# Score products one couple ahead of their transposed partners, and two late pieces of the last group moved

## The chip, the cores and the metric

The kernel runs on one core of a Trainium2 chip. The metric is the device time of one launch in microseconds, the median of several runs; profiles are of one execution. The engines are PE (matrix products), DVE, ACT and POOL (elementwise work) and SP (transfers only), and PE's matrix array can be used as one block of 128 rows or, for operands that span 64 partitions, as two halves of 64 rows. In this text L is the half of rows 0 to 63 and U that of rows 64 to 127.

## The reference

```python
S, D, H, Dh, W, F = 2048, 512, 32, 16, 256, 1792

q, k, v = split_heads(x @ wqkv)                      # 32 heads of 16
scores = einsum("bhqd,bhkd->bhqk", q, k) * Dh**-0.5
mask = (i - j >= 0) & (i - j < W)                    # sliding block
p = softmax(where(mask, scores, -1e9))
a = merge_heads(einsum("bhqk,bhkd->bhqd", p, v)) @ wo

b = (silu(x @ w_gate) * (x @ w_up)) @ w_down

g = sigmoid((x * gate_w).sum(-1, keepdims=True))
out = g * a + (1 - g) * b
```

## The kernel before

Float32 operands are split into two parts, hi and lo, and each product is made of three (hi by hi, hi by lo, lo by hi). A prologue makes v and the projections q and k. A last stage multiplies the hidden tiles by `w_down` and the attention's output by `wo`. The change lies in the stage between, which runs attention and the products with `w_gate` and `w_up` side by side.

That stage goes through the 32 heads in 8 groups of 4. It has 128 blocks t (16 per group, one for each 128 queries), and each block has four couples hd = 0 to 3; a couple is the unit of its order, number 4t + hd. In a couple the loop at L796 issues, in this order:

- one score product of the next group (L593, `stage1`, a generator that yields after each): queries by keys, 384 columns wide, from which DVE takes the row maxima (L595) that the softmax of the next group subtracts;
- one transposed score product of this group (L632, `stage2`): keys by queries, whose exponentials ACT makes (L634), and which POOL then masks (L636, L639). In the last group, from block 112 (`g7`) on, no next group is left, and `stage2` gives two products in couples 0 and 2;
- one to three steps of the stream of gate and up products (L554, `lanes`). A step is one product on L (lane 0) and one on U (lane 1), each 512 columns wide. `DEAL` sets how many steps a couple gets;
- what is entered for that couple in a table of pieces of work, by `at` and `later`.

A head's score product lies on L when its number in the group is even, and on U when it is odd. `stage1` takes heads in the order 0, 1, 2, 3, and `stage2` in the order 1, 0, 3, 2. So the two products of a couple lie on different halves before: L and U, U and L, L and U, U and L.

Every fourth block begins with value products (`av`, L654: 48 products of 64 rows by 32 columns, over a chunk of 512 queries). They are issued in couple 1, after its steps. Before the change couple 1 then has one more score product, that of head 2, just ahead of the value products, and couple 2 has none. `evacuate` follows: ACT copies the second half of the sums out (L665) and DVE or POOL adds it to the first.

PSUM has three banks in turn for score products (they wait for DVE, L595, three products back) and two for transposed ones (they wait for ACT, L634, two products back); the value products take one turn of each.

In the last group more is woven in. Three hidden tiles for the last stage are made early: tiles 0 and 1 by `tile_early`, whose six pieces (exponential on ACT; add, reciprocal and two products on DVE; the split into halves on ACT and DVE) are entered for the couples counted from block 122 in the table at L777. For chunks 0 and 1 the softmax denominators are read back from DRAM, inverted and written again by `invert`: a read on POOL's queue (L456), a reciprocal on DVE (L458), a write on POOL's queue (L460), at the couples set in L764 to L766. The read of a chunk waits for the transfer of that chunk's values, which `evacuate` issues four couples after the value products.

The loop's lines around the two generators:

```python
s1 = stage1(g + 1, i) if t < g7 else iter(())
s2 = stage2(g, i) if t < G * NB else iter(())
if not (values and hd == 2):
    run(s1, 1)
```

Of the kernel before, what the change touches and what calls it, by code (L numbers as in the profile page):

```python
# [19 lines left out]
NB = S // P  # L20
CH = 512
NCH = S // CH
G = H // 4
# [10 lines left out]
def gated_mix(ctx, tc, xT, xn, wqk, wv, wo, wgu, wd, gw, out):  # L34
# [52 lines left out]
    def run(gen, n=None):  # L87

        while n is None or n > 0:
            if next(gen, run) is run:  # L90
                break
            n = n and n - 1
# [19 lines left out]
    def bank(n):  # L112
        names = BANKS[n if isinstance(n, str) else ("pa", "pb", "pc", "pd")[n]]
        names.append(names.pop(0))
        return psum.tile([P, CH], F32, name=names[-1])
# [338 lines left out]
    def invert(c, pool):  # L454
        den = pool.tile([P, P], F32, name="den")
        nc.gpsimd.dma_start(den, shares[:, c * CH:(c + 1) * CH].rearrange("h (q i) -> h q i", q=4))  # L456
        yield
        nc.vector.reciprocal(den, den)  # L458
        yield
        nc.gpsimd.dma_start(rd[c].rearrange("h (q i) -> (h q) i", q=4), den)  # L460
        yield
# [7 lines left out]
    with ExitStack() as A:  # L469
# [14 lines left out]
        def at(k, *fs):  # L484
            AT.setdefault(k, []).extend(fs)
# [4 lines left out]
        def tick_end():  # L490
            for f in AT.pop(NOW[0], ()):
                f()
# [88 lines left out]
        def stage1(g, qb):  # L581

            hf, b = divmod(qb, NB // 2)
            if b == 0:
                MX[g, hf] = sm.tile([P, 4, NB // 2], F32, name="mx")
            q0, k0 = qb * P, max(0, qb - 2) * P
            n = q0 + P - k0
            for hd in range(4):
                pr, j = divmod(hd, 2)
                r = slice(64 * j, 64 * j + 63)  # L590

                ps = bank("pd") if g == 0 and pr else bank("pc")
                nc.tensor.matmul(ps[:, :n], QT[g % 2][pr][r, q0:q0 + P], KT[g % 2][pr][r, k0:k0 + n],  # L593
                                 start=True, stop=True)
                mx = nc.vector.tensor_tensor_reduce(out=ps[:, :n], in0=ps[:, :n], in1=mask[:, 3 * P - n:],  # L595
                                                    scale=1.0, scalar=NEG, op0=ALU.add, op1=ALU.max,
                                                    accum_out=MX[g, hf][:, hd, b:b + 1])
                if g == 0:
                    BEHIND.append(mx)
                yield  # L600
# [129 lines left out]
        def tile_load(n, place):  # L730
            GOT[n] = [h.bitcast(F32) for h in halves_of(pieces[place])]
            for i in range(2):
                nc.sync.dma_start(GOT[n][i], raws[n, i, 0])
# [21 lines left out]
        g7 = (G - 1) * NB  # L755
# [6 lines left out]
        at(4 * (g7 + 2), gate_end)  # L762
        INV = [invert(c, osb) for c in range(2)]
        for c in range(2):  # L764
            for n in (0, 12, 15):
                at(4 * (g7 + 5 + 4 * c) + 3 + n, lambda c=c: run(INV[c], 1))  # L766
        at(4 * g7, put_pieces)
        def put_back():
            PART.append(osb.tile([P, D], F32, name="xn", bufs=2))
# [4 lines left out]
            wd_early(4 * (g7 + 1 + m) + 2, m, m)  # L774
        for n in range(2):
            at(4 * (g7 + 9) + 1 + n, lambda n=n: tile_load(n, RAW_AT[n]))
        for n, ticks in enumerate(((1, 3, 3, 3, 3, 12), (7, 9, 9, 9, 9, 15))):  # L777
            early = tile_early(n)
            for m in ticks:
                at(4 * (g7 + 10) + m, lambda early=early: run(early, 1))  # L780
# [12 lines left out]

        DEAL = [[[(hd + 1) * n // 4 - hd * n // 4 for hd in range(4)] for n in deal] for deal in ((4, 9, 9, 8), (8, 8, 8, 8))]
        DEAL[0][0] = 1, 1, 2, 0
        for t in range(G * NB + 1):  # L796
            g, i = divmod(t, NB)
            d, part = divmod(t, NSLOT)
            s1 = stage1(g + 1, i) if t < g7 else iter(())
            s2 = stage2(g, i) if t < G * NB else iter(())  # L800
            values = part == 0 and t > 0
            for hd in range(4):
                k = NOW[0] = NSLOT * t + hd
                if not (values and hd == 2):
                    run(s1, 1)
                if t < g7:
                    run(s2, 1)
                elif hd % 2 == 0:
                    run(s2, 2)
                if t == G * NB and hd == 0:  # L810
                    last_tile = tile_silu(2)
                    run(last_tile, 1)
                if t < G * NB:
                    run(steps, DEAL[t >= g7][part][hd])
                if hd == 1 and values:
                    run(s1, 1)
                    av(*divmod(d - 1, NCH))
                    while UNDER:
                        UNDER.pop(0)()
                    evacuate(*divmod(d - 1, NCH))  # L820
                tick_end()
            if i in (7, 15) and g + 1 < G:
                UNDER.append(lambda g=g, i=i: put_max(g + 1, i // 8))
            if t >= 10 and t % 4 == 2 and t + 6 < G * NB:
                load_v((t + 6) // 4)
# [196 lines left out]
```

## Time and profile before

| | |
|---|---|
| median of 3 runs | 839.43 us (839.18 to 839.72) |
| the profiled execution, its own time | 840.21 us |
| the profiled execution, span | 838.5 us, mean granted clock 0.992 |
| busy: PE, DVE, ACT, POOL | 829.0, 554.9, 471.7, 400.3 us |
| blocks 0 to 111 (transposed products of groups 0 to 6) | 216.44 to 576.87 us of the span |
| the last group | 576.87 to 637.70 us |
| the last stage | 637.70 to 838.5 us |

A row of a timeline has the start in microseconds from the span's start, the duration, the engine, the line, the operation, and the tile that is written and those that are read; then the size, and in brackets how long the engine sat idle before and what released it. Rows of the products' durations overlap, since they are pipelined; the time that a product costs its half is the distance to the next start on that half. The tiles `pc`, `pb` and `pd` of L593 and L632 are their PSUM banks. In a row of stages the first number is the stage's length, then each engine's busy time, and PEclk is the share of the full clock that was granted to PE.

### The profile page before, as it was taken

The page shows a single profiled execution, that of the slowest core. Times are in us where ns is not written, and L with a number is a line of the kernel's source. Part 1 is how long each engine was busy: PE and PEld are TensorE (multiplying, and loading weights), DVE is VectorE, ACT ScalarE, POOL GpSimd, SP SyncE. Part 2 cuts the span into 40 slices and gives each one's busy share as a digit, 9 for nine tenths or more (in the row PEclk, how much of TensorE's full clock was granted, in tenths as well). Part 3 has the DMA queues.
Part 4 walks back from the last instruction along what each step waited for, and adds up shares of the span by engine and source line. Part 5 has one row for each costly group of instructions (what it writes and reads, how often), then busy time and mean ns, then how long its engine had stood idle before and what let it go on. Part 6 is the DMA issues. An engine that isn't in the chain of part 4 may idle for free.

```text
span 838.5 us, 20514 instructions
## 1 busy us (share of the span) xinstructions
PE 829.0 (99%) x7681; PEld 703.8 (84%) x7681; DVE 554.9 (66%) x1425; ACT 471.7 (56%) x956; POOL 400.3 (48%) x715
## 2 busy tenths in 40 slices
PE   9999999999999999999999999999989999999997
PEld 7888888888898888888888888888767888888886
DVE  5675554258787887878878778784493657554652
ACT  7454453222576766767767667676665564434341
POOL 5124441341365765766667666666673115342220
PEclk9999999999999999999999999999997999999999
DMA  8456666385534664545655455433637897868611
GB/s 297 143 173 228 226 257 229 132 271 187 193 109 148 210 191 156 188 159 204 198 163 190 156 166 182 162 116 115 222 123 260 308 277 237 261 220 248 214 51 50
DMA packets 80211, 159.70 MB, mean 190 GB/s; under 512 B 14960, under 2 KB 19440, under 8 KB 80112
## 3 DMA queue, kind: packets, MB, share of 16 engines
q1 hardware_dynamic: 68544, 127.44, 45.7%
q0 software_dynamic: 10992, 29.91, 10.9%
q8 instruction: 60, 0.98, 0.5%
q10 hardware_dynamic: 576, 1.05, 0.4%
q14 instruction: 39, 0.32, 0.1%
HBM read 93.32 MB, written 65.01 MB: 189 GB/s over the span
## 4 chain that ended last, share of the span: by engine, by line
PE 97%; DVE 1%; ACT 1%; DMA 1%; POOL 0%; issue 0%; DVEq 0%; ACTq 0%; POOLq 0%
PE pa L554 21%; PE pb L554 10%; PE pd L632 7%; PE pc L654 4%; PE pd L381 4%; PE pb L381 4%; PE pa L381 4%; PE pc L593 3%; PE pd L654 3%; PE pd L81 3%; PE pc L83 3%; PE pc L82 3%; PE pd L82 3%; PE pd L83 3%; PE pc L81 3%; PE pb L654 2%
## 5 line engine op out<-in xcount | busy, mean ns | idle before, releaser
L634 ACT ACTIVATE pt<-pd 128x384 f32<-128x384 f32 (+2 forms) x512 | 232.3, 474 | 52.5 <-PE pd L632 12.2
L595 DVE CUSTOM_DVE_ANT_0 pc<-pc,mask 128x384 f32<-128x384 f32 (+2 forms) x322 | 172.8, 547 | 39.5 <-PE pc L593 20.3
L632 PE MATMUL pd<-q,k 64*128 64x384 f32 (+2 forms) x512 | 177.1, 358 | 2.9 <-ACT pt L634 2.7
L554 PE MATMUL pa<-xhi,wl 64*128 64x512 f32 x492 | 161.7, 399 | 0.0
L554 PE MATMUL pa<-xlo,wh 64*128 64x512 f32 x492 | 160.1, 397 | 0.0
L554 PE MATMUL pa<-xhi,wh 64*128 64x512 f32 x492 | 159.0, 396 | 0.0
L636 POOL TENSOR_SCALAR_AFFINE_SELECT pt<-pt 128x256 f32<-128x256 f32 x256 | 108.1, 423 | 77.6 <-ACT pt L634 75.6
L632 PEld LDWEIGHTS pd<-q,k 64*128 64x128 f32 x512 | 93.9, 185 | 25.8 <-ACT pt L634 9.9
L593 PE MATMUL pc<-k,q 63*128 63x384 f32 (+2 forms) x322 | 103.3, 327 | 0.0
L554 PE MATMUL pb<-xhi,wl 64*128 64x512 f32 x244 | 97.2, 398 | 0.0
L554 PE MATMUL pb<-xlo,wh 64*128 64x512 f32 x244 | 96.7, 396 | 0.0
L554 PE MATMUL pb<-xhi,wh 64*128 64x512 f32 x244 | 96.3, 395 | 0.0
L595 DVE CUSTOM_DVE_ANT_0 pb<-pb,mask 128x384 f32<-128x384 f32 (+2 forms) x158 | 86.8, 549 | 14.0 <-PE pb L593 8.6
L639 POOL TENSOR_SCALAR_AFFINE_SELECT pt<-pt 128x256 f32<-128x256 f32 x224 | 95.7, 427 | 0.0
L554 PEld LDWEIGHTS pa<-xhi,wl 64*128 64x128 f32 x492 | 81.1, 186 | 1.5
L554 PEld LDWEIGHTS pa<-xhi,wh 64*128 64x128 f32 x492 | 80.1, 186 | 2.5 <-DVE mx L595 0.5
L554 PEld LDWEIGHTS pa<-xlo,wh 64*128 64x128 f32 x492 | 80.0, 186 | 1.4
L595 DVE DVE_READ_ACCUMULATOR2_ANT mx<- 128x1 f32 x512 | 72.3, 141 | 0.0
L907 DVE TENSOR_TENSOR sg<-got,sg 128x512 f32<-128x512 f32 x53 | 41.8, 788 | 45.6 <-ACT sg L906 39.8
L654 PE MATMUL pd<-pt,vg 64*32 64x320 f32 (+4 forms) x1184 | 62.9, 345 | 0.0
L593 PEld LDWEIGHTS pc<-k,q 63*128 63x128 f32 x322 | 58.7, 184 | 4.9 <-issue 0.4
L672 POOL TENSOR_TENSOR oe<-oe,ob 128x512 f32<-128x512 f32 (+1 forms) x28 | 35.1, 1252 | 52.0 <-ACT ob L665 48.7
(305 smaller groups left out, 2064.1 us busy)
## 6 DMA issues: line engine op xcount, KB each, us to landing
got<-raws SPq DMA_DIRECT2D x106, 256.0 KB
raws<-ev SPq DMA_DIRECT2D x91, 256.0 KB
q<-xd SPq DMA_DIRECT2D x96, 128.0 KB
k<-xd SPq DMA_DIRECT2D x96, 128.0 KB
xd<-cx SPq DMA_DIRECT2D x16, 512.0 KB
xd<-cy SPq DMA_DIRECT2D x16, 512.0 KB
od<-oe POOLq DMA_DIRECT2D x32, 256.0 KB, 3.2
raw<-wgu SPq DMA_DIRECT2D x25, 256.0 KB
```

The source lines that it names most:

```text
L81: nc.tensor.matmul(ps, lh, rh, start=start and i == 0, stop=False, skip_group_check=skip)
L82: nc.tensor.matmul(ps, lh, rl, start=False, stop=False, skip_group_check=skip)
L83: nc.tensor.matmul(ps, ll, rh, start=False, stop=stop and i == n - 1, skip_group_check=skip)
L381: nc.tensor.matmul(ps, l[:, w], r[:, k], start=n in (1, 2, 5) and k == m == 0, stop=k == 1 and m == 2, skip_group_check=True)
L554: mm = nc.tensor.matmul(ps[o], w[r], x[r], start=first and i == 0, stop=(o is odd or bool(lane)) and i == turn - 1)
L593: nc.tensor.matmul(ps[:, :n], QT[g % 2][pr][r, q0:q0 + P], KT[g % 2][pr][r, k0:k0 + n], start=True, stop=True)
L595: mx = nc.vector.tensor_tensor_reduce(out=ps[:, :n], in0=ps[:, :n], in1=mask[:, 3 * P - n:], scale=1.0, scalar=NEG, op0=ALU.add, op1=ALU.m ...
L632: nc.tensor.matmul(ps[:, :n], KT[g % 2][pr][r, k0:k0 + P], QT[g % 2][pr][r, k0:k0 + n], start=True, stop=True)
L634: BEHIND.append(nc.scalar.activation(pt[:, j, :n], ps[:, :n], AF.Exp, scale=SCALE))
L636: nc.gpsimd.affine_select(out=pt[:, :, :P], in_=pt[:, :, :P], pattern=[[0, 2], [1, P]], compare_op=ALU.is_ge, fill=0.0, base=0, channel_mu ...
L639: nc.gpsimd.affine_select(out=pt[:, :, 2 * P:], in_=pt[:, :, 2 * P:], pattern=[[0, 2], [-1, P]], compare_op=ALU.is_ge, fill=0.0, base=-1, ...
L654: nc.tensor.matmul(AV[g, c][h][32 * j:32 * j + 32, q0 - c * CH:q1 - c * CH], VG[4 * g + kb // 4][o, kb % 4, 17 * j:17 * j + 32], PT[g, kb, ...
```

## The change

All score products of groups 1 to 7 now come from one generator, `scores`. One is issued ahead of block 0, and then one in each couple, with no exception around the value products. So each couple has the score product that stood one couple later before, except that the one just ahead of the value products now stands at the beginning of that couple. The heads of a couple are now 1 and 1, 2 and 0, 3 and 3, 0 and 2: both products of a couple lie on the same half, U, L, U, L.

In the last group the denominators of chunks 0 and 1 are read two blocks (8 couples) later, inverted 8 instead of 12 couples after the read and written 11 instead of 15 after it. The halves of early tile 1 are split in couple 19 instead of 15, counted from block 122.

```diff
-            for n in (0, 12, 15):
-                at(4 * (g7 + 5 + 4 * c) + 3 + n, lambda c=c: run(INV[c], 1))
+            for n in (0, 8, 11):
+                at(4 * (g7 + 7 + 4 * c) + 3 + n, lambda c=c: run(INV[c], 1))
...
-        for n, ticks in enumerate(((1, 3, 3, 3, 3, 12), (7, 9, 9, 9, 9, 15))):
+        for n, ticks in enumerate(((1, 3, 3, 3, 3, 12), (7, 9, 9, 9, 9, 19))):
...
+        scores = chain(*(stage1(*divmod(b, NB)) for b in range(NB, G * NB)))
+        run(scores, 1)
         for t in range(G * NB + 1):
             g, i = divmod(t, NB)
             d, part = divmod(t, NSLOT)
-            s1 = stage1(g + 1, i) if t < g7 else iter(())
             s2 = stage2(g, i) if t < G * NB else iter(())
             values = part == 0 and t > 0
             for hd in range(4):
                 k = NOW[0] = NSLOT * t + hd
-                if not (values and hd == 2):
-                    run(s1, 1)
+                run(scores, 1)
                 if t < g7:
                     run(s2, 1)
                 elif hd % 2 == 0:
...
                 if hd == 1 and values:
-                    run(s1, 1)
                     av(*divmod(d - 1, NCH))
```

**PE, block 60, up to the first value product.** L593 is the score product, L632 the transposed one, L554 a step's two products. Before:

```order
L593 MATMUL pc_5961<-k_1366,q_1346 128x384
L632 MATMUL pd_5965<-q_1502,k_1504 128x384
L554 MATMUL pb_5921<-xhi_95,wh 128x512
L554 MATMUL pa_5840<-xhi_93,wh 128x512
L593 MATMUL pc_5971<-k_1366,q_1346 128x384
L632 MATMUL pd_5974<-q_1502,k_1504 128x384
L554 MATMUL pb_5921<-xlo_96,wh 128x512
L554 MATMUL pa_5840<-xlo_94,wh 128x512
L593 MATMUL pb_5981<-k_1414,q_1388 128x384
L654 MATMUL pc_5984<-pt,vg 32x320
```

Now:

```order
L593 MATMUL pc_5964<-k_1366,q_1346 128x384
L632 MATMUL pd_5968<-q_1502,k_1504 128x384
L554 MATMUL pb_5924<-xhi_95,wh 128x512
L554 MATMUL pa_5843<-xhi_93,wh 128x512
L593 MATMUL pb_5974<-k_1414,q_1388 128x384
L632 MATMUL pd_5977<-q_1502,k_1504 128x384
L554 MATMUL pb_5924<-xlo_96,wh 128x512
L554 MATMUL pa_5843<-xlo_94,wh 128x512
L654 MATMUL pc_5984<-pt,vg 32x320
```

The lone score product between the last step and the value products has moved into the couple; the two rows of a couple read alike but are of other heads (1 and 1, then 2 and 0).

**PE, block 60, after the last value product.** Before:

```order
L632 MATMUL pd_6043<-q_1514,k_1516 128x384
L554 MATMUL pb_5921<-xhi_95,wl 128x512
L554 MATMUL pa_5840<-xhi_93,wl 128x512
L554 MATMUL pb_5921<-xhi_95,wh 128x512
L554 MATMUL pa_5840<-xhi_93,wh 128x512
L593 MATMUL pc_6052<-k_1414,q_1388 128x384
L632 MATMUL pd_6055<-q_1514,k_1516 128x384
L593 MATMUL pb_6060<-k_1366,q_1346 128x384
L632 MATMUL pd_6064<-q_1502,k_1504 128x384
```

Now:

```order
L593 MATMUL pc_6042<-k_1414,q_1388 128x384
L632 MATMUL pd_6046<-q_1514,k_1516 128x384
L554 MATMUL pb_5924<-xhi_95,wl 128x512
L554 MATMUL pa_5843<-xhi_93,wl 128x512
L554 MATMUL pb_5924<-xhi_95,wh 128x512
L554 MATMUL pa_5843<-xhi_93,wh 128x512
L593 MATMUL pb_6055<-k_1366,q_1346 128x384
L632 MATMUL pd_6058<-q_1514,k_1516 128x384
L593 MATMUL pc_6063<-k_1366,q_1346 128x384
L632 MATMUL pd_6067<-q_1502,k_1504 128x384
```

Couple 2, which had no score product, now has that of head 3, and each later couple that of the head after.

**ACT, blocks 125 to 127.** The row `CAST q` is the first half of early tile 1's split, which waits for DVE; L634 is an exponential. Before:

```order
L634 ACTIVATE pt<-pd_10091 128x384
L69 CAST q_1514<-ev 128x512
L634 ACTIVATE pt<-pd_10115 128x256
L634 ACTIVATE pt<-pd_10118 128x256
L501 COPY ev<-pa_9918 128x512
L634 ACTIVATE pt<-pd_10135 128x256
L634 ACTIVATE pt<-pd_10138 128x256
L634 ACTIVATE pt<-pd_10154 128x128
```

Now:

```order
L634 ACTIVATE pt<-pd_10090 128x384
L634 ACTIVATE pt<-pd_10112 128x256
L634 ACTIVATE pt<-pd_10115 128x256
L501 COPY ev<-pa_9915 128x512
L634 ACTIVATE pt<-pd_10132 128x256
L634 ACTIVATE pt<-pd_10135 128x256
L69 CAST q_1514<-ev 128x512
L634 ACTIVATE pt<-pd_10154 128x128
```

The cast has moved past the four exponentials of block 126 and a copy. On POOL the read of chunk 0's denominators has moved past eight masks (two blocks), that of chunk 1 likewise. The write of chunk 1 has moved behind three loads of `w_down` (L785) and two masks of block 126; it still stands ahead of block 127's masks. On DVE each reciprocal of a denominator (L458) has moved behind the next split, one or two rows.

## The prediction

> **What bounds the kernel now.** First I read the page's busy times and its row of the granted clock.
>
> ```profile
> PE 829.0 (99%) x7681; PEld 703.8 (84%) x7681; DVE 554.9 (66%) x1425; ACT 471.7 (56%) x956; POOL 400.3 (48%) x715
> PEclk9999999999999999999999999999997999999999
> ```
>
> PE is busy all through, so the time can only come from products that cost less, or from PE's waits. One slice shows a lower clock. The row of stages, asked for around that slice, shows both kinds of loss:
>
> ```profile
> 625.00:628.00 3.00, 0.66 (x6) 0.23 (x3) 2.93 (x5) 1.04 (x3) 0.65 (x2) 0.99 0.39 158
> 628.00:632.00 4.00, 4.00 (x18) 3.66 (x19) 1.62 (x3) 1.63 (x6) 2.75 (x6) 0.50 0.40 98
> 632.00:636.00 4.00, 4.00 (x52) 1.85 (x58) 0.11 (x1) 2.94 (x5) 2.51 (x6) 0.50 0.78 311
> 636.00:640.00 4.00, 4.00 (x65) 2.92 (x50) 1.88 (x3) 1.11 (x2) 0.58 (x2) 0.73 0.27 81
> 637.70:838.50 200.80, 196.36 (x872) 162.57 (x867) 111.70 (x153) 85.47 (x150) 56.41 (x72) 0.99 0.67 214
> ```
>
> Between 625 and 628 PE works 0.66 of 3 us, and then it has half its clock (0.50, 0.50, 0.73 granted) for some ten microseconds. The last stage behind it is PE at work again (196.36 of 200.80 us), so what is won ahead of it passes through. The timelines of PE, ACT and DVE say who stopped PE:
>
> ```profile
> 625.19 0.39 PE L554 MATMUL pb<-xlo,wh 64*128 64x512 f32 x1
> 627.91 0.85 PE L632 MATMUL pd<-q,k 64*128 64x256 f32 x2 [2.34 <-ACT pt L634]
> 623.27 0.94 ACT L634 ACTIVATE pt<-pd 128x384 f32<-128x384 f32 x2
> 626.96 0.62 ACT L69 CAST q<-ev 128x512 fp32r<-128x512 f32 x1 [2.74 <-DVE ev L742]
> 621.99 3.35 DVE L740 RECIPROCAL ev<-ev 128x512 f32<-128x512 f32 x1
> 626.23 0.69 DVE L742 TENSOR_TENSOR ev<-q,ev 128x512 f32<-128x512 f32 x1
> 626.84 0.94 DVE L458 RECIPROCAL den<-den 128x128 f32<-128x128 f32 x1
> ```
>
> ACT stands 2.74 us at the cast of early tile 1, because DVE's chain for it (a reciprocal of 3.35 us, then two products) ends at 626.92. Queued behind the cast are block 126's exponentials, and PE's next transposed pair needs their banks: it starts at 627.91.
>
> Within the long stage I read PE's timeline around one set of value products (block 60), from the last couple before them to the second after them:
>
> ```profile
> 408.86 0.34 PE L593 MATMUL pc<-k,q 63*128 63x384 f32 x1
> 408.87 0.33 PE L632 MATMUL pd<-q,k 64*128 64x384 f32 x1
> 409.04 0.39 PE L554 MATMUL pb<-xlo,wh 64*128 64x512 f32 x1
> 409.27 0.33 PE L593 MATMUL pb<-k,q 63*128 63x384 f32 x1
> 409.56 0.43 PE L654 MATMUL pc<-pt,vg 64*32 64x320 f32 x1
> ...
> 412.17 0.44 PE L632 MATMUL pd<-q,k 64*128 64x384 f32 x1
> 412.90 0.33 PE L593 MATMUL pc<-k,q 63*128 63x384 f32 x1
> 413.00 0.44 PE L632 MATMUL pd<-q,k 64*128 64x384 f32 x1
> 413.28 0.34 PE L593 MATMUL pb<-k,q 63*128 63x384 f32 x1
> 413.39 0.44 PE L632 MATMUL pd<-q,k 64*128 64x384 f32 x1
> 414.13 0.33 PE L593 MATMUL pc<-k,q 63*128 63x384 f32 x1
> 414.30 0.40 PE L554 MATMUL pa<-xhi,wh 64*128 64x512 f32 x2
> ```
>
> Two products on different halves start together (408.86, 408.87). A score or transposed product costs its half 0.17 us (409.04 less 408.87), a step's product 0.23 (409.27 less 409.04). The score product at 409.27 stands alone: half U has nothing until the value products at 409.56, 0.29 us later, of which 0.17 are that product's own.
>
> **The change, part by part.** *Same halves.* Now both products of a couple lie on one half, U, then L. If PE kept strictly to program order, the other half would idle. Whether it does so, the start of the stream of lanes shows, where lane 0 runs alone. The program has there three step products on L, then a score on L into `pb`, then a score on U into `pc`:
>
> ```profile
> 180.86 0.39 PE L554 MATMUL pb<-xhi,wh 64*128 64x512 f32 x1
> 180.86 0.44 PE L593 MATMUL pc<-k,q 63*128 63x384 f32 x1
> 181.09 0.39 PE L554 MATMUL pb<-xlo,wh 64*128 64x512 f32 x1
> 181.32 0.39 PE L554 MATMUL pb<-xhi,wl 64*128 64x512 f32 x1
> 181.55 0.34 PE L593 MATMUL pb<-k,q 63*128 63x384 f32 x1
> ```
>
> The score on U, fifth in order, starts at 180.86 with the first of L's four: four places ahead, and 0.69 us before the one that precedes it. So the halves run apart by up to four unstarted products. I walk the new order with that: score on U at 0, transposed on U at 0.17, L's first step product at 0 (two places ahead), its second at 0.23, U's at 0.34 and 0.57; then L's score at 0.46 and transposed at 0.63, and both halves meet at 0.80 with two couples' work balanced after 1.26 us, as before (2 x 0.17 + 4 x 0.23 = 1.26). No step needs more than four places. So 448 couples cost nothing extra, if the look-ahead holds; if it did not at all, two couples would cost 0.17 more, since the step products of L wait for the transposed product on U. Price from both sides: 0, or 224 x 0.17 = 38 us. I take 0, since the row is of the same two kinds of product on the same halves.
>
> A rule speaks against this. The Trainium skill (TensorE: Matmul & The Clock Gate, Part 3, "The mechanism") says that matmuls start and end in program order, strictly first in, first out, also between row groups. This trace does not agree: of the two scores above the later one in the program starts 0.69 us sooner. By the rule the sum would be the second price.
>
> *The lone score.* It joins a couple, at 27 sets of value products (blocks 4 to 108). In 21 of them it is 384 wide (0.17), in the 6 at a group's first block 128 wide (a third, 0.06). Behind the value products, what binds is ACT and DVE:
>
> ```profile
> 412.36 0.59 ACT L665 COPY ob<-pd 128x512 f32<-128x512 f32 x1 [2.33 <-PE pd L654]
> 412.84 1.58 ACT L634 ACTIVATE pt<-pd 128x384 f32<-128x384 f32 x3
> 412.31 0.69 DVE L671 COPY oe<-pc 128x512 f32<-128x512 f32 x1 [1.19 <-POOL pt L639]
> 413.27 0.56 DVE L595 CUSTOM_DVE_ANT_0 pc<-pc,mask 128x384 f32<-128x384 f32 x1 [0.26 <-PE pc L593]
> ```
>
> The transposed products at 413.00 and 413.39 wait for ACT's copy and first exponential, 0.83 and 1.22 us after 412.17; that stays, since the copy is released by the value products. Now scores of heads 3 and 0 fill U and L before 0.83, the next score needs the bank that DVE copies until 413.00 (0.83 again, so nothing new waits), and after 1.22 two steps and the score of head 2 follow: L reaches the next steps at about 1.22 + 2 x 0.23 + 2 x 0.17 = 2.02, against 2.13 before (414.30 less 412.17), with one score more done. So the gain is the score itself: 21 x 0.17 + 6 x 0.06 = 3.9 us. From both sides: 0, if the earlier scores meet DVE or ACT somewhere else, and 27 x 0.35 = 9.5, if the whole 0.29 and a little of the wait after 412.17 go. DVE's three score banks are one couple less slack: a score waits for the one three back, 1.9 us earlier at two couples in 1.26, and DVE is done with it some 0.9 us after its start (the score of 412.90 is taken at 413.27, for 0.56). One solo score at block 0 costs 0.06.
>
> *Early tile 1.* The cast moves past block 126's exponentials, so PE's pair at 627.91 can follow the step product at 625.19 after 0.23: 2.5 us are won. If the clock does not drop, the half clock goes too: 4 x 0.50 + 4 x 0.50 + 4 x 0.27 = 5.1 us. Given back: the cast still waits for DVE until 626.96 and takes 0.6, and queued behind it are now block 127's exponentials. PE reaches that block's first pair at about 626.4 and its second at 627.4; the second needs the first's exponentials, which end at about 627.9 (626.96 + 0.62, and 0.3 for one that is 128 wide, where two of 384 take 0.94), so 0.5 us are lost. Block 127's masks then stand on POOL behind the denominators' write, which waits for a split and the reciprocal on DVE until about 628.5 (626.92 + 0.69 + 0.94); the value products need them only in their last rounds, for which I add 0.3. Net 7.6 - 0.8 = 6.8 us.
>
> *The denominators' reads.* The row of POOL's wait and that of what it held up:
>
> ```profile
> 603.19 0.56 POOL L456 DMA_DIRECT2D den<-od  x1 [4.22 <-DMA od<-oe]
> PEld pc L654 <- POOL pt L636: 1.5, 3, 0.7
> ```
>
> POOL stood 4.22 us for the values' transfer with eight masks behind it; in this group the value products waited for masks 1.5 us in all (three times). Now the masks stand ahead of the read. Between 0 and 1.5 I take 0.8. The other moves (reciprocals behind a split on DVE) lie beside PE's work, since their results are read in the last stage.
>
> **Sum.** 3.9 + 6.8 + 0.8 = 11.5 us off the profiled span of 838.5, which leaves 827.0. That execution's own time is 840.21, 0.8 above the runs' median of 839.43; the median should go to 839.4 - 11.5 = 827.9.
>
> **Rivals.** *Halves in order (slower).* If a waiting product on one half holds the other back, each two couples lose up to 0.17 us: 839.4 + 38 - 7.6 = 870. It decides against the change from a fifth of that on (7.6 / 224 = 0.034 us in two couples). For it: every transposed product carries a wait for ACT, and what stands behind a waiting product can't start, as after 625.19. Against it: the rows at 180.86. One in ten.
>
> *The clock drops anyway.* Block 127 keeps short stops with one lane alone. Then 5.1 of the 6.8 stay: 839.4 - 3.9 - 0.8 - 1.7 = 833.0. For it: the stop that dropped the clock lasted only 2.5 us; against it: the stage in which POOL stood 4.22 us kept the full clock:
>
> ```profile
> 600.00:610.00 10.00, 9.63 (x151) 7.16 (x153) 5.15 (x9) 5.64 (x14) 5.75 (x14) 1.00 0.93 324
> ```
>
> One in eight. The Trainium skill (TensorE: Matmul & The Clock Gate, Part 1, "What's actually happening") gives an idle window of 3.4 us for the drop. Here 2.5 us of idle time were enough.
>
> *The scores win nothing*, because they only reach ACT's and DVE's waits sooner: 839.4 - 7.6 = 831.8, one in five. *They win all* at the value products: 839.4 - 9.5 - 7.6 = 822.3, one in eight.
>
> **Numbers.** Forecast 0.45, halves in order 0.10, clock 0.12, nothing won 0.20, all won 0.13. The likeliest gives 828. The bounds of the terms (9.5 + 7.6 + 1.5) reach down to 821, and with a little for what the walk leaves out 819; upwards 838 takes in the clock and a loss of some 0.01 us per couple, and leaves out halves in order. About 0.2% (1.7 us) is what a measurement can tell from no change: faster 0.87, within it 0.03, slower 0.10.
>
> **What would show it.** Right: the cast of early tile 1 behind block 126, no stage of 0.50 granted clock, the first value product some 0.35 after the last step products, and a cycle of four blocks shorter by about 0.17. Wrong: in couples far from value products, step products of one half 0.4 us apart where 0.23 or 0.17 stood; or score products that wait for DVE. The prediction fails if the couples themselves change their price.

## The result and the profile after

The change makes the kernel faster: 832.52 us, median of 4 runs (831.70 to 834.11), against 839.58 for the kernel before (839.18 to 839.96). The ratio is 0.9918, with a 95% interval of 0.9901 to 0.9936. The forecast was 828.0 with a range of 819 to 838: right in sign and inside the range, but of the 11.5 us of its sum only 7.1 came. The experiments show that the sum was also composed otherwise than the prediction had it.

The profiled execution after took 831.7 us, span 830.0. From its page, the busy times and the granted clock:

```profile
PE 821.3 (99%) x7681; PEld 692.9 (83%) x7681; DVE 553.9 (67%) x1425; ACT 472.0 (57%) x956; POOL 400.9 (48%) x715
PEclk9999999999999999999999999999999999999999
```

The slice with a lower clock is gone. To see where the time went I cut both spans at the same four events: the first transposed product of blocks 0, 120 and 124, and the first product of the last stage (L81). The row of blocks 0 to 111 ends at block 112's first transposed product. Columns as before: stage, its length, busy time of PE, PEld, DVE, ACT and POOL, granted clock, share of the transfer engines, GB/s. Before:

```profile
216.44:576.87 360.43, 360.38 (x4943) 319.10 (x4944) 288.49 (x984) 254.84 (x563) 234.91 (x491) 1.00 0.50 164
602.15:616.13 13.98, 13.55 (x180) 10.21 (x176) 8.14 (x10) 9.73 (x23) 9.23 (x22) 1.00 0.62 215
616.13:637.71 21.58, 19.24 (x266) 13.30 (x263) 13.99 (x13) 10.98 (x26) 14.14 (x31) 0.77 0.41 141
637.71:838.50 200.79, 196.35 (x871) 162.57 (x867) 111.70 (x153) 85.47 (x150) 56.41 (x72) 0.99 0.67 214
```

After:

```profile
216.09:573.48 357.39, 357.32 (x4943) 311.28 (x4943) 289.84 (x986) 254.57 (x563) 232.35 (x491) 1.00 0.50 165
598.78:611.97 13.19, 13.13 (x180) 10.16 (x176) 8.89 (x11) 9.72 (x23) 10.58 (x20) 1.00 0.66 228
611.97:626.98 15.01, 14.80 (x266) 10.76 (x263) 10.60 (x12) 10.95 (x26) 12.25 (x27) 1.00 0.50 170
626.98:830.00 203.02, 196.72 (x871) 162.21 (x867) 112.68 (x154) 85.90 (x151) 56.91 (x73) 1.00 0.69 214
```

Blocks 0 to 111 are 3.04 us shorter, blocks 120 to 123 0.79, and the stretch from block 124 to the last stage 6.57. The start of block 0 is 0.35 earlier, blocks 112 to 119 are the same (25.28 and 25.30). But the last stage, in which nothing was changed, is 2.23 longer. The sum, 0.35 + 3.04 - 0.02 + 0.79 + 6.57 - 2.23, is the 8.5 us by which the spans differ. The medians differ by 7.1, since the profiled execution before lay 0.6 above its median (840.21 against 839.58), and the one after 0.8 below its own.

**Early tile 1.** ACT's timeline, then PE's, in the profile after:

```profile
622.81 0.62 ACT L69 CAST q<-ev 128x512 fp32r<-128x512 f32 x1 [0.61 <-DVE ev L742]
```

```profile
623.06 0.39 PE L554 MATMUL pa<-xhi,wh 64*128 64x512 f32 x1
623.66 0.49 PE L632 MATMUL pd<-q,k 64*128 64x128 f32 x2 [0.21 <-ACT pt L634]
```

The cast now holds ACT for 0.61 us where it held it for 2.74, and PE's longest wait for an exponential there is 0.21 where it was 2.34.

**The last stage.** PE's timeline in the profile after, at the fourth hidden tile, the first that was not made early:

```profile
635.05 0.39 PE L83 MATMUL pc<-q,k 128*128 128x512 f32 x1
635.75 0.50 PE L81 MATMUL pd<-q,hh 128*128 128x512 f32 x1 [0.32 <-ACT hh L69]
636.09 0.40 PE L82 MATMUL pd<-q,hh 128*128 128x512 f32 x1
638.00 0.50 PE L83 MATMUL pd<-q,hl 128*128 128x512 f32 x1 [1.51 <-DVE hl L72]
```

Products of this stage follow each other at 0.23 us (635.05 less 634.82, the start ahead of it). Here two come late, by 0.47 and by 1.68 us (638.00 less 636.09 is 1.91). DVE's timeline says why:

```profile
633.97 0.69 DVE L906 TENSOR_TENSOR sg<-got,sg 128x512 f32<-128x512 f32 x1 [4.74 <-DMA got<-raws]
636.65 0.69 DVE L906 TENSOR_TENSOR sg<-got,sg 128x512 f32<-128x512 f32 x1 [1.39 <-DMA got<-raws]
637.26 0.68 DVE L72 TENSOR_TENSOR hl<-sg,hh 128x512 fp32r<-128x512 f32 x1
```

The stage's first hidden tiles are loaded from DRAM (`got`), and their loads are issued when the last value products are done. They land late: DVE waits 4.74 us for one and 1.39 for the next, and PE waits for ACT and DVE. Two rows show the transfer engines in the 2 us ahead of the last stage, before and after (the last number but one is their busy share):

```profile
635.71:637.71 2.00, 2.00 (x65) 1.18 (x49) 0.69 (x1) 0.15 (x1) 0.00 (x0) 0.50 0.18 68
```

```profile
624.98:626.98 2.00, 2.00 (x91) 1.38 (x73) 0.55 (x1) 1.97 (x3) 2.00 (x6) 1.00 0.78 316
```

While PE worked at half clock before, earlier transfers ran dry, and the loads met engines that were 0.18 busy. Now they meet 0.78. In f1 below, which has the half clock too, the share is 0.43, and PE does not wait there either; in the twelve profiles with the full clock ahead of the last stage it is 0.78 to 0.95. Two loads of `w_down` run beside the `got` loads, before as well as after: the first of them is issued 2.2 us into the stage before and 2.3 us now.

### The profile page after: what moved, and what is told of

The parts are those of the page before. It is cut to its first block, busy times and chain, and to the rows that moved or that the text cites. A ratio compares the mean times of both kernels' runs of the same rounds, so it can differ in the third digit from the quotient of the medians.

```text
span 830.0 us, 20514 instructions
## 1 busy us (share of the span) xinstructions
PE 821.3 (99%) x7681; PEld 692.9 (83%) x7681; DVE 553.9 (67%) x1425; ACT 472.0 (57%) x956; POOL 400.9 (48%) x715
## 3 DMA queue, kind: packets, MB, share of 16 engines
q10 hardware_dynamic: 576, 1.05, 0.4%
## 4 chain that ended last, share of the span: by engine, by line
PE 96%; DMA 1%; DVE 1%; ACT 1%; SPq 0%; issue 0%; DVEq 0%; ACTq 0%
PE pa L554 22%; PE pb L554 11%; PE pd L632 7%; PE pc L654 4%; PE pd L381 4%; PE pb L381 4%; PE pa L381 4%; PE pd L654 3%; PE pd L83 3%; PE pc L82 3%; PE pc L83 3%; PE pc L81 3%; PE pd L82 3%; PE pd L81 3%; PE pb L654 2%; PE pc L381 2%
## 5 line engine op out<-in xcount | busy, mean ns | idle before, releaser
L634 ACT ACTIVATE pt<-pd 128x384 f32<-128x384 f32 (+2 forms) x512 | 231.9, 474 | 47.8 <-PE pd L632 26.1
L632 PE MATMUL pd<-q,k 64*128 64x384 f32 (+2 forms) x512 | 173.1, 350 | 0.7 <-ACT pt L634 0.6
L554 PE MATMUL pa<-xlo,wh 64*128 64x512 f32 x492 | 167.9, 397 | 0.0
L554 PE MATMUL pa<-xhi,wl 64*128 64x512 f32 x492 | 167.5, 394 | 0.0
L554 PE MATMUL pa<-xhi,wh 64*128 64x512 f32 x492 | 167.5, 392 | 0.0
L632 PEld LDWEIGHTS pd<-q,k 64*128 64x128 f32 x512 | 94.2, 185 | 27.5 <-ACT pt L634 11.5
L593 PE MATMUL pc<-k,q 63*128 63x384 f32 (+2 forms) x322 | 107.0, 337 | 0.0
L554 PE MATMUL pb<-xlo,wh 64*128 64x512 f32 x244 | 97.0, 397 | 0.0
L554 PE MATMUL pb<-xhi,wl 64*128 64x512 f32 x244 | 96.1, 394 | 0.0
L554 PE MATMUL pb<-xhi,wh 64*128 64x512 f32 x244 | 95.5, 392 | 0.0
L554 PEld LDWEIGHTS pa<-xhi,wh 64*128 64x128 f32 x492 | 87.6, 185 | 2.0 <-DVE mx L595 0.5
L554 PEld LDWEIGHTS pa<-xhi,wl 64*128 64x128 f32 x492 | 88.1, 185 | 1.1
L554 PEld LDWEIGHTS pa<-xlo,wh 64*128 64x128 f32 x492 | 87.4, 185 | 0.7
L593 PEld LDWEIGHTS pc<-k,q 63*128 63x128 f32 x322 | 58.6, 184 | 5.0 <-issue 3.5
```

The source lines that it names most:

```text
L554: mm = nc.tensor.matmul(ps[o], w[r], x[r], start=first and i == 0, stop=(o is odd or bool(lane)) and i == turn - 1)
L632: nc.tensor.matmul(ps[:, :n], KT[g % 2][pr][r, k0:k0 + P], QT[g % 2][pr][r, k0:k0 + n], start=True, stop=True)
L634: BEHIND.append(nc.scalar.activation(pt[:, j, :n], ps[:, :n], AF.Exp, scale=SCALE))
```

## The experiments

All stages come from profiles cut at the same events. Medians of the kernel before, in the three sessions: 839.41 (e1, e2, e5, e7), 839.25 (e3, e4, e6, e8) and 839.38 us (f1 to f4).

| | median | ratio and interval | blocks 0-111 | 120-123 | 124 to last stage | last stage |
|---|---|---|---|---|---|---|
| before | 839.58 | | 360.43 | 13.98 | 21.58 | 200.79 |
| the change | 832.52 | 0.9918 (0.9901-0.9936) | 357.39 | 13.19 | 15.01 | 203.02 |
| e1 scores only | 836.82 | 0.9973 (0.9959-0.9987) | 357.85 | 14.24 | 17.32 | 202.74 |
| e2 last group only | 836.53 | 0.9955 (0.9936-0.9975) | 360.49 | 13.19 | 15.02 | 202.61 |
| e3 early tile only | 838.02 | 0.9994 (0.998-1.0007) | 360.36 | 13.48 | 17.09 | 205.54 |
| e4 denominators only | 838.23 | 1.0002 (0.9984-1.0019) | 360.34 | 13.18 | 17.68 | 203.26 |
| e5 other halves | 834.45 | 0.9949 (0.9932-0.9965) | 359.87 | 13.18 | 15.02 | 202.16 |
| e6 step before values | 835.43 | 0.9955 (0.9937-0.9973) | 358.83 | 13.19 | 15.04 | 203.69 |
| e7 step after values | 826.51 | 0.986 (0.9837-0.9882) | 351.79 | 13.18 | 15.00 | 203.59 |
| e8 loads later | 830.72 | 0.9895 (0.988-0.9909) | 357.27 | 13.18 | 15.03 | 201.25 |
| f1 same half only | 836.34 | 0.9961 (0.9949-0.9973) | 357.19 | 14.20 | 20.51 | 200.98 |
| f2 step and loads | 825.37 | 0.9834 (0.9814-0.9855) | 351.65 | 13.20 | 15.02 | 202.67 |
| f3 six steps | 827.70 | 0.9864 (0.9844-0.9884) | 354.30 | 13.19 | 15.03 | 201.93 |
| f4 tile and loads | 838.71 | 0.9995 (0.9982-1.0008) | 360.35 | 14.54 | 17.09 | 201.89 |

In four profiles in which neither scores nor heads were touched (e2, e3, e4, f4) blocks 0 to 111 lie within 0.1 us of the 360.43 of before, so 0.5 us in this column is more than chance.

### The change in its parts: e1 to e4

**e1: the scores alone.** The change, with the last group's table as before:

```diff
-            for n in (0, 8, 11):
-                at(4 * (g7 + 7 + 4 * c) + 3 + n, lambda c=c: run(INV[c], 1))
+            for n in (0, 12, 15):
+                at(4 * (g7 + 5 + 4 * c) + 3 + n, lambda c=c: run(INV[c], 1))
...
-        for n, ticks in enumerate(((1, 3, 3, 3, 3, 12), (7, 9, 9, 9, 9, 19))):
+        for n, ticks in enumerate(((1, 3, 3, 3, 3, 12), (7, 9, 9, 9, 9, 15))):
```

> Only the order of the score products is changed; the last group stays as before. If the couples keep their price and the lone score is won at the value products, blocks 0 to 111 (216.44 to 576.87 us before) are shorter by 3.0 to 3.4 us as in the changed kernel, the stop at early tile 1 and the half clock stay, and the time is 839.6 - 3.4 = 836.2. If the scores win nothing and all of the 7.1 us come from the last group, 839.6.

836.82 us, 2.6 below its before, near what was expected. Its profile held a surprise, in PE's timeline and three rows of stages:

```profile
625.40 0.66 PE L632 MATMUL pd<-q,k 64*128 64x256 f32 x2 [2.35 <-ACT pt L634]
```

```profile
622.00:625.00 3.00, 1.06 (x9) 0.62 (x7) 2.93 (x4) 0.55 (x2) 1.13 (x3) 1.00 0.45 180
625.00:628.00 3.00, 2.60 (x19) 2.33 (x20) 2.11 (x4) 2.11 (x8) 2.05 (x4) 1.00 0.27 56
628.00:632.00 4.00, 4.00 (x103) 2.69 (x103) 0.86 (x2) 3.58 (x7) 3.21 (x8) 1.00 0.78 298
```

The stop is there as before (2.35 us against 2.34), yet the clock stays at 1.00. So the half clock of the first profile is not a sure consequence of the stop. e4 shows the same: a wait of 2.36 us and the full clock. f1, further down, has the same wait and the half clock. How these executions differ stands in the last section.

**e2: the last group alone** (the rest of the diff undone: scores as before, the three lines of the last group as in the change).

> Only the last group's pieces are moved (early tile 1's halves, the denominators); the scores stay as before. The last group should lose 7.3 us as in the changed kernel and the last stage should then wait about 2.2 us for its first loaded hidden tile: 839.6 - 7.3 + 2.2 = 834.5. If the last stage's wait came from the scores' order, there would be none and the time would be 832.3. If the two parts need each other, more than 836.

836.53 us, 2 us more than expected. The gain ahead of the last stage is there in full (21.58 to 15.02, 13.98 to 13.19), but the last stage takes 202.61. (Its profiled span, 834.8, also has 1.8 us more ahead of block 0 than that of before, in a part that no edit touches: 3.41 us there are at half clock, from 7.79 us on.)

**e3: early tile 1 alone.** The kernel before with one number changed:

```diff
-        for n, ticks in enumerate(((1, 3, 3, 3, 3, 12), (7, 9, 9, 9, 9, 15))):
+        for n, ticks in enumerate(((1, 3, 3, 3, 3, 12), (7, 9, 9, 9, 9, 19))):
```

> Only early tile 1's halves are split four couples later; scores and denominators as before. The stop before 627.91 and the half clock should go (7.6 us less 0.8 to 1.0 given back), the value products of block 120 should still wait for masks, and the last stage should wait some 2 us: 839.6 - 6.7 + 2.2 = 835.1. If the denominators' move is what frees ACT, no change: 839.6.

A miss: 838.02, no change that can be told. The stop of 2.5 us is gone, but 17.09 us from block 124 on is no better than the 17.32 of e1, which has the stop and no half clock. POOL's timeline, then PE's, show what came in its place:

```profile
624.73 0.42 POOL L639 TENSOR_SCALAR_AFFINE_SELECT pt<-pt 128x256 f32<-128x256 f32 x1
627.59 0.56 POOL L460 DMA_DIRECT2D rd<-den  x1 [2.44 <-DVE den L458]
629.21 0.54 POOL L785 DMA_DIRECT2D wl<-wd  x1
629.76 0.77 POOL L636 TENSOR_SCALAR_AFFINE_SELECT pt<-pt 128x256 f32<-128x256 f32 x2
```

```profile
630.23 0.40 PE L654 MATMUL pc<-pt,vg 64*32 64x256 f32 x1 [0.78 <-POOL pt L636]
```

POOL stands 2.44 us at the denominators' write, for a reciprocal that DVE makes behind the tile; the three loads of `w_down` and block 127's masks come after it, and the value products wait for the masks. From the first to the last start of these value products it is 4.34 us, in the change and in e2 2.28: that is all of the 2.07 us by which the stretch is longer than in e2 (17.09 against 15.02). In the change the denominators' pieces are later too, and there is no such wait:

```profile
623.61 0.77 POOL L636 TENSOR_SCALAR_AFFINE_SELECT pt<-pt 128x256 f32<-128x256 f32 x2
624.54 0.56 POOL L460 DMA_DIRECT2D rd<-den  x1 [0.16 <-issue]
```

**e4: the denominators alone** (the kernel before with the first pair of lines of e1's diff turned round).

> Only the denominators are moved; early tile 1 and the scores as before. The value products of block 120 should take 2.5 instead of 3.26 us, and the rest stays: 839.6 - 0.8 = 838.8. If they had a part in the stop at early tile 1 (the reciprocal stands behind it on DVE), up to 7 us less.

838.23, no difference, near what was expected. Blocks 120 to 123 take 13.18, 0.80 less than in the profile before. In the nine profiles with this move the stretch takes 13.18 to 13.20, in the five without it 13.48 to 14.54: the wait for the transfer was of varying length, and the move ends it.

The two late pieces are worth more together than apart. Without a half clock the stretch from block 124 on takes 17.32 with neither (e1), 17.09 with the tile, 17.68 with the denominators, and 15.02 with both (e2).

### Lone score or same half: e5, e6, f1

**e5: the lone score into the couple, the couple on two halves.** The change, with the heads of the score products in another order from group 1 on, so that a couple's two products lie on different halves as before:

```diff
-            for hd in range(4):
+            for hd in range(4) if g == 0 else (1, 0, 3, 2):
```

> The changed kernel with the scores of groups 1 to 7 in the order of heads 1, 0, 3, 2, so that the two products of a couple lie on different halves again while the scores stay one couple ahead. If the halves run apart and only each half's total work counts, 832.5 within 1.5. If products on one half cost something in a couple (0.01 us or more), 828 or less.

834.45, 1.9 slower than the change and just above the interval expected. The row of blocks 0 to 111:

```profile
216.39:576.26 359.87, 359.83 (x4943) 314.83 (x4943) 286.55 (x986) 255.48 (x563) 233.50 (x491) 1.00 0.51 164
```

Of the 3.04 us that the change gains there, 0.56 are left. That speaks against the prediction, in which the whole gain of these blocks comes from the lone score and none from the halves. f1 turns the test round.

**f1: the same half, the lone score left where it was.** The same line as in e5, in the kernel before.

> The kernel before, with one edit: from group 1 on the score products take the heads in the order 1, 0, 3, 2. Then both products of a couple lie on one half, as in the change, while the lone score ahead of the value products and the last group stay as before. In the profiles of the change the step products (L554) start 0.227 us apart on their half, where before, and in the run with the other halves, it is 0.233. Theory 'the halves win': that comes from the couples lying on one half; here too it is 0.227, groups 1 to 6 (blocks 16 to 111, 311.28 us before, 310.51 with the other halves, 308.33 in the change) take about 311.28 - (310.51 - 308.33) = 309.1 us, and the median falls by 2.2 us to about 837.1. Theory 'the lone score wins' (the prediction's): the couples' price is the same on one half or two, the stretch stays at 311.3 and the median at 839.3.

836.34, 3.0 faster than before, and the row:

```profile
216.28:573.47 357.19, 356.88 (x4944) 305.58 (x4944) 296.40 (x984) 254.31 (x563) 235.86 (x491) 1.00 0.51 165
```

3.24 us are gained by the order of heads alone, which puts each couple on one half: as much as the change gains in these blocks. It comes in plain blocks too. Two starts on PE, the first transposed products of blocks 67 and 68 (eight steps and four couples between them), before:

```profile
431.58 0.33 PE L632 MATMUL pd<-q,k 64*128 64x384 f32 x1
434.15 0.34 PE L632 MATMUL pd<-q,k 64*128 64x384 f32 x1
```

and in f1:

```profile
429.70 0.34 PE L632 MATMUL pd<-q,k 64*128 64x384 f32 x1
432.23 0.34 PE L632 MATMUL pd<-q,k 64*128 64x384 f32 x1
```

2.57 us became 2.53. I took the distance from each start of a step product between 260 and 570 us of the span to the next start on its half, where that follows after 0.20 to 0.26 us and is no value product. (The rows do not name the half; I inferred it from the times at which each half is due.) The mean is 0.2325 us before (1,283 of them) and 0.2326 in e5 (1,282), but 0.2293 in the change (1,305) and 0.2291 in f1 (1,309). All six versions with couples on two halves lie at 0.2323 to 0.2326, and the eight with couples on one half at 0.2291 to 0.2304. A half has 840 step products in these blocks (30 in four blocks, 28 times); 840 x 0.0034 = 2.9 us, most of f1's gain. Why a step product costs 0.0034 us less is open: it hangs little on what the other half starts in the meantime (in the change 0.2290 with a step, 0.2298 with a score, 0.2294 with a transposed product).

**e6: a step ahead of the value products.** The change, with one of the steps of the block's third couple moved into its second, ahead of the value products:

```diff
-        DEAL[0][0] = 1, 1, 2, 0
+        DEAL[0][0] = 1, 2, 1, 0
```

> The changed kernel with one step of the stream moved from couple 2 to couple 1, so that the value products begin 0.23 us later. In the changed kernel they take 0.2 us longer than before in three of four blocks. If that is a wait for ACT and for masks, they should be as short as before (2.5 for 48 and 2.0 for 32 products), and the time be about the same, 832.5 within 2. If they are slower for themselves, they stay at 2.75 and 2.21.

835.43, slower than expected. It shows what became of the lone score. In 27 sets of value products, from the first of them to the product behind the last, the mean is 2.40 us before, 2.54 in the change, 2.55 in e5, and 2.38 here. Waits of PE's weight loads in blocks 0 to 111, before and then in the change (total us, times, longest):

```profile
PEld pc L654 <- POOL pt L639: 1.0, 3, 0.3
```

```profile
PEld pc L654 <- POOL pt L636: 3.7, 12, 0.3
PEld pd L654 <- ACT pt L634: 3.0, 15, 0.2
PEld pb L654 <- POOL pt L636: 1.9, 6, 0.3
```

The lone score had covered a wait: without it the value products begin 0.18 us sooner (0.32 us behind the last step product instead of 0.50, in the mean of the 27) and then take 0.14 longer, for masks and exponentials. That they are short again with a step in its place (2.38) is what the expectation had asked of a wait. The rows of waits name the engines but do not measure the loss: the weight loads still wait 5.2 us for masks in e6. Blocks 0 to 111 take 358.83 there, 1.4 longer than the change; the likely reason is that the couple behind the value products lacks that step, where e7 finds idle time.

### Idle time behind the value products: e7, f3

**e7: a step moved behind them.** The change, with one step of the second block of four moved into the last couple of the first:

```diff
-... for deal in ((4, 9, 9, 8), (8, 8, 8, 8))]
-        DEAL[0][0] = 1, 1, 2, 0
+... for deal in ((5, 8, 9, 8), (8, 8, 8, 8))]
+        DEAL[0][0] = 1, 1, 2, 1
```

> The changed kernel with one step of the stream moved from the block after the value products' block into couple 3 behind the value products, where two transposed products wait for ACT (0.83 and 1.22 us after the value products). If PE's halves idle there and can be filled, 27 times up to 0.2 us: 827.5. If the wait only moves on to the next transposed product, 832.5.

826.51, the largest gain of one edit, and as expected:

```profile
216.33:568.12 351.79, 351.72 (x4943) 307.96 (x4943) 291.14 (x986) 252.17 (x563) 232.29 (x491) 1.00 0.53 168
```

351.79 against 357.39: 5.6 us, or 0.21 for each of 27 sets, about what a step product costs its half (0.23). The halves did stand idle behind the value products: with the costs above, a half has about 0.31 us of idle time between 1 and 2 us behind the start of the last value product in the change, and 0.09 here.

**f3: two steps moved.** As f2 below, with `((6, 8, 8, 8), ...)` and `1, 1, 2, 2`.

> As the kernel with the step and the loads moved, but with a second step moved into the block that begins with the value products (6, 8, 8, 8 steps in four blocks where it has 5, 8, 9, 8; couple 3 has two). If what is left of PE's idle time around the value products (0.30 to 0.45 us in four blocks, with a step moved) is of the same kind, 0.1 us for each of 27: 824.7 - 2.7 = 822 us. If what is left are the value products' own waits for masks (POOL L636), the step fills nothing: 824.7. If the third block with 8 steps instead of 9 then waits for ACT's exponentials, it is slower, 826 or more.

827.70, slower than f2: the third case. The wait of weight loads of transposed products for ACT's exponentials in f2, then in f3:

```profile
PEld pd L632 <- ACT pt L634: 4.1, 21, 0.4
```

```profile
PEld pd L632 <- ACT pt L634: 10.1, 52, 0.3
```

The block that gave up its ninth step now runs into ACT: 5.9 of the 10.1 us lie in the third block of four, where f2 has no such wait.

### The last stage: e8, f2, f4

**e8: two loads out of the way.** The change, with the loads of two rows of `w_down` moved from the beginning of the last stage to the place of the next such load, behind it in POOL's order:

```diff
-... ((13, "raw"), (13, "wh"), (13, "wl"), (17, "wh"), (17, "wl")), 8):
+... ((13, "raw"), (13, "wh"), (13, "wl")), 8):
...
                     nc.gpsimd.dma_start(WDRAW[13], wd[13])
+                    wd_raw(11, "wh")
+                    wd_raw(12, "wl")
```

> The changed kernel with two loads of w_down rows (11 and 12, 256 KB each) issued some 7 us later in the last stage, out of the stretch in which the first hidden tile is loaded. If that load is late because the transfers share the engines, the wait of 2.2 us in step 3 shrinks by 0.5 MB of the traffic, to 1 or less: 831. If it is late by its own latency, 832.5.

830.72, as expected: 1.8 less than the change, and the last stage takes 201.25, 1.77 less. PE's waits for the first hidden tiles have shrunk to one, of 0.17 us:

```profile
636.26 0.50 PE L83 MATMUL pd<-q,hl 128*128 128x512 f32 x1 [0.17 <-DVE hl L72]
```

So the transfers that run beside the first loads have a part in their lateness, in the place where the prediction had seen no wait. How large a part these two loads have is less sure than the match suggests: f2 and f3, with the same two loads moved, take 202.67 and 201.93 us for the last stage, and e5, without, 202.16. Between e7 and f2 the loads are worth 1.1 us of the median.

**f2: e7 and e8 together.**

> The change, with a step moved behind the value products and the two loads of w_down moved into the last stage, the two edits that each made it faster alone (826.51 and 830.72 against 832.52). If the two waits are separate (the idle time behind the value products and the last stage's first loads), the sum: 826.5 - 1.8 = 824.7 us, with no wait over 0.5 us in the first 20 us of the last stage. If the earlier start of the last stage brings another load onto the path, 826.5 as with the step alone.

825.37, the fastest version, 14 us below its before; 0.7 above the sum, as a wait of the last stage is left:

```profile
630.60 0.50 PE L81 MATMUL pd<-q,hh 128*128 128x512 f32 x1 [0.86 <-ACT hh L69]
```

**f4: early tile 1 and the loads.** e3, with the two loads of e8 put in, but one line higher, ahead of the load that they stand behind in e8.

> The kernel before, with early tile 1's halves moved as in the change and two loads of w_down moved into the last stage; scores and denominators as before. With the halves alone the median was 838.02 (ratio 0.9994), though the stop of 2.5 us is gone, and its profile has two new places: 2.5 us of waits for the last stage's first loads (L81 for ACT, L83 for DVE), and 1.4 us of waits of the last value products for masks, which stand on POOL behind the denominators' write and three loads of w_down. Theory 'given back behind it': the loads' place gives most of the first back, and with two loads fewer ahead of block 127's masks (0.54 us each on POOL) also about 1 us of the second: 838.0 - 1.8 - 1.0 = 835.2 us. Theory 'the halves' move was worth nothing': 838.0.

838.71, no change, and no test of the theory: that next load waits on POOL (issued at 641.41 us), and the two ahead of it do not (636.01, 2.3 us into the last stage, as in the change). Nor are they the loads ahead of block 127's masks, as the expectation had it. What the run does show is e3 over again: 17.09 us from block 124 to the last stage, with 1.1 us of waits for masks. Its last stage takes 201.89 us with the loads in their old place.

## Why the prediction came out as it did

**The step that failed.** "So what is won ahead of it passes through." The last stage gave back 2.23 us of the 10.7 won ahead of it. The sentence rested on PE being busy 196.36 of 200.80 us in the profile before. It was so busy where the half clock ahead of it had let the transfers run dry. In the two profiles with the half clock there the last stage takes 200.79 (before) and 200.98 (f1), and PE waits for no load in its first 25 us. With the full clock ahead of it and the two loads in their old place it takes 201.89 to 203.69 in eight profiles, and 201.25 to 202.67 in the three with the loads moved (e8, f2, f3). e3, at 205.54, has a stretch of half clock of its own there.

**The half clock.** The term that holds it was sized right for the profiled execution: 6.57 against the 6.8 forecast. But the half clock was taken as a property of the kernel. Without it (e1) the stretch takes 17.32, and the last stage 202.74: of the 4.26 us that the half clock costs there, 1.95 come back at once. So early tile 1 and the denominators together are worth 2.3 us there in an execution with full clock, and a net 2.3 more in one in which the clock drops. Of the 61 runs of the kernel before beside the experiments, the 13 with a mean granted clock of 0.999 or more have a median of 837.65 us, the other 48 one of 839.49; the mean does not say where the clock fell. The change's three runs at 0.999 or more have a median of 832.38, which is 5.3 us less where the medians of all runs differ by 7.1. The rival "the clock drops anyway" did not come true, but its opposite, that the clock need not have dropped before, was not among the rivals. The row brought against that rival says nothing on it: where POOL stood 4.22 us, PE worked 9.63 of 10 us, so PE had no stop there.

**What the cast gives back.** Forecast at 0.8, partly for masks behind the denominators' write. In the change there is nothing of it: the denominators' edit moves that write behind three loads and two masks, and there POOL does not stand for it (0.16 us of idle time against 2.44 in e3). Alone, the tile's move pays 2.06 us (e3). The prediction added the two edits up, but the tile's move needs the other.

**The lone score.** Forecast at 3.9 us, measured at 0.56 (e5), and at nothing beside the same halves (357.39 against 357.19 in f1). The sentence that failed is "So the gain is the score itself": the value products begin 0.18 us sooner and take 0.14 us longer, a cost that the walk did not have. The rival "the scores win nothing, because they only reach ACT's and DVE's waits sooner" had the mechanism nearly right: what they reach are the value products' waits for POOL and ACT.

**The couples.** Forecast at 0, with +38 as the other bound, measured at -3.24 (f1). The walk was right that PE does not hold one half back for the other. The Trainium skill (TensorE: Matmul & The Clock Gate, Part 3, "The mechanism") has matmuls start and end in program order; with couples on one half that would have cost up to 38 us by the prediction's working, and f1 is 3.0 us faster. But no bound below nothing was put to this price, and by chance it came out at the size of the term that failed: 3.04 us against 3.9 in these blocks looks like a near hit, and only e5 and f1 show that it is two misses. The signs that the prediction named for being right could not show it. The first value product starts 0.32 us behind the last step product, where it named 0.35; and four blocks are 0.14 us shorter (12.84 against 12.98, blocks 20 to 111), where it named 0.17. Its last sign of being wrong did come: the couples themselves changed their price, though downwards.

**The denominators' reads.** Forecast at 0.8, measured at 0.79 (13.98 to 13.19), within the bounds of 0 and 1.5.

In sum, between the two profiles: 3.9 became 3.04 from another cause, 6.8 became 6.57, more than half of it a clock that falls in some executions only, 0.8 became 0.79, 0.35 us came at the start, and 2.23 us went back. That the time came out inside the range is in part luck.

## What to carry to other kernels

A stage that looks bound by its own work may be so only because the stage ahead of it is slow: before counting a gain as passed through, look which transfers the later stage starts with, and whether they were landing in the time that is to be removed. A loss that hangs on the clock should be looked for in a second execution before its price goes into a sum. And a term that comes out near its forecast is not yet understood: two experiments that split it, one with each half of the edit, cost little and showed here that the credit belonged to the other half.

## What the hardware showed

**The clock's drop comes and goes, and lasts for whole multiples of 3.41 us.** After stops of the same length (waits of 2.34, 2.35, 2.36 and 2.36 us before, in e1, e4 and f1) the granted clock fell to 0.50 before and in f1, and not in e1 and e4. Three stretches of half clock, before, in f1 and in e3's last stage:

```profile
627.92:638.16 10.24, 10.24 (x117) 7.00 (x118) 2.39 (x4) 5.00 (x12) 5.26 (x11) 0.50 0.46 162
```

```profile
625.67:632.50 6.83, 6.83 (x65) 4.35 (x69) 1.00 (x3) 3.83 (x9) 4.63 (x10) 0.50 0.69 240
```

```profile
644.54:647.95 3.41, 3.41 (x9) 2.67 (x10) 3.41 (x7) 2.82 (x6) 0.74 (x2) 0.50 1.04 395
```

10.24, 6.83 and 3.41 us are three, two and one times 3.41, and the one at the start of e2 lasts 3.41 as well. The changes of the clock lie on one grid: before, from its rise at 6.70 us to its drop at 627.92 it is 182 times 3.4133 us, and in each profile all later changes are whole multiples of 3.413 us from the first. So each profile can be cut into windows of 3.41 us. The window ahead of the drop, before; then the two windows over which the stop is spread in e1, and the two in e4:

```profile
624.51:627.92 3.41, 1.07 (x10) 0.64 (x8) 3.34 (x5) 0.96 (x3) 1.13 (x3) 1.00 0.38 154
```

```profile
620.89:624.30 3.41, 2.17 (x19) 1.53 (x15) 3.34 (x3) 0.81 (x3) 2.24 (x6) 1.00 0.45 181
624.30:627.71 3.41, 2.31 (x17) 2.04 (x18) 2.81 (x5) 2.67 (x8) 1.76 (x4) 1.00 0.19 41
```

```profile
622.89:626.30 3.41, 1.84 (x15) 1.21 (x12) 3.34 (x4) 0.65 (x3) 2.42 (x6) 1.00 0.49 172
626.30:629.71 3.41, 2.62 (x19) 2.35 (x20) 2.50 (x4) 2.50 (x9) 0.96 (x2) 1.00 0.16 59
```

Where the clock fell, all of the idle time lay in one window (in e3 that of two waits), and PE worked 1.07 of its 3.41 us before, 1.05 in f1 and 0.92 in e3. Where it did not fall, the edge of a window cut the stop in two, and PE worked 1.84 us or more in each. So in these runs the drop goes with the place of the stop on the grid, and the grid lies otherwise in each execution (its first change is at 6.70 us before, 6.49 in e1, 5.08 in e4 and 4.45 in f1). No single limit fits all of them: at the start of e2 the clock fell after a window with 1.87 us of work. The Trainium skill (TensorE: Matmul & The Clock Gate, Part 1, "What's actually happening") has the clock follow a window of 3.4 us that runs free of the kernel. The lengths agree with that, and so does a stop that drops the clock in one execution and not in another. The Trainium skill asks there for one idle window; these stops were shorter than that.

**Two products on one half are cheaper than one on each.** The step products around them started 0.2291 us apart in f1 and 0.2325 before, and blocks 0 to 111 were 3.24 us shorter. The cause is open.
